# Val products of the last five batches by seven block products, sums on VectorE, last factor on GpSimd, v by casting DMAs

## Chip, cores and metric

The kernel runs on one core of one Trainium2 chip. The metric is the time of one execution on the device in microseconds (us). Engines carry the names of the profile: PE is TensorE, with PEld for its weight loads, DVE is VectorE, ACT is ScalarE, POOL is GpSimd and SP is SyncE. SBUF is the on-chip memory, PSUM the banks into which PE writes. "val" below is the product with w_val, "g" that with w_gate.

## What is computed

An attention with a sigmoid in place of the softmax, whose heads are laid side by side, and a gated feed-forward block behind it:

```python
batch, n_heads, seq, head_dim = (8, 12, 448, 64)
...
n_tokens, d_model, d_ff = (3584, 768, 1536)
...
    scores = scale * np.matmul(q, k.transpose(0, 1, 3, 2)) - np.log(S)
    attn = 1.0 / (1.0 + np.exp(-scores))
    return np.matmul(attn, v).astype(np.float32)
...
    g = x @ w_gate
    silu = g * (1.0 / (1.0 + np.exp(-g)))
    val = x @ w_val
    return (silu * val @ w_out).astype(np.float32)
```

## The kernel before

**Attention.** A block i (24 of them, 3 per batch) holds four heads. `load` (L252) brings its q, k and v in float32 into staging buffers `st`, through the DMA queue of SP. `cast_qk` (L269) makes 16-bit copies in `src`, mostly on POOL, and `cast_v` (L284) makes v in fp16 by three POOL casts; `load_v` (L293), which would load v by DMAs on POOL's queue that cast on the way, is used for i >= `VDMA`, and with `VDMA = 24` for no block. q and k are transposed into `qkT`, by PE for the first six blocks (`tr_pe`) and by a transposing DMA on SP's queue for the rest (`tr_dma`). `burst` (L387) makes one or two of a block's seven score tiles in the two PSUM buffers with the tag A, and ACT turns each into `pt` by a sigmoid. `pv` (L419) multiplies by v into two TO banks, and two copies put the result as fp16 tiles `xT` of 128 x 448 into SBUF, six per batch (768 rows of x transposed, 448 tokens).

**Feed-forward, first half.** `f1` (L461) makes, for a batch b and a block f of 128 of the 1536 hidden columns, g (six matmuls of 128 x 128 weights and 448 columns) and val (six more), each in a PSUM bank with the tag G. There are two G banks, taken in turn; for the last batch val goes to A instead. ACT takes the sigmoid of g, DVE multiplies it with g to `t1` (L482), and DVE multiplies val with t1 and a scale to `hT` (L488). Twelve f per batch, eight batches.

**Feed-forward, second half.** For each pair of batches m, `f2_set` (L608) makes the product with w_out by seven block products in place of eight (the Winograd form of Strassen's scheme): sums of hT blocks (`s`), weight sums made once by `weight_sums` (L582) in part of the staging buffers, products in TO banks (and A at the end), and adds into `osb` on DVE. `f2` (L518) makes the rest plainly. Stores go through POOL's queue while attention runs, through SP's at the end.

**Order.** The order is written out by a planner. Every step is an `Op` with an engine, an assumed duration, the steps it depends on, and the buffer tags that it takes and gives back. `list_schedule` (L64) runs through assumed time; on PE it picks the first step that is ready among the next 40, on DVE among 16, on ACT 12, on POOL 8, on SP strictly in order. Buffers of one tag are taken in the order in which the steps were listed. Each engine then executes its instructions in the order so found. In the main loop (L780 to L840) block i's attention is listed together with about one f per quarter block of the batch before and with f2 steps. `NEARLY = 5` staging buffers serve the loads after the early ones; the other six then hold the weight sums of f2.

Of the kernel before, what the change touches and what calls it, by code (L numbers as in the profile page):

```python
# [9 lines left out]
FP32 = mybir.dt.float32  # L10
FP16 = mybir.dt.float16
# [47 lines left out]
VDMA = 24  # L59
# [94 lines left out]
def kernel(  # L154
# [33 lines left out]
             "v16": 3, "qkT": 3, "pt": 10, "xT": 14, "osb": 3, "osf": 4, "S": 2}  # L188
# [6 lines left out]
    wide = one.tile([128, 512], BF16, tag="wide", name="wide")  # L195
    nc.vector.memset(wide, 0.0)
# [4 lines left out]
    NEARLY = 5  # L201
# [8 lines left out]
    stt = [stg.tile([128, 2 * NS * D], FP32, tag=f"st{n}", name=f"st{n}") for n in range(slots["st"])]  # L210

    def wsum(j, c, n=1):

        x = (j - 1) * NH + c
        o = x % 4 * HW
        return stt[NEARLY + x // 4].bitcast(FP16)[:, o:o + n * HW]
# [22 lines left out]
    def buffer(n):  # L239

        return n % len(stt) if n < uses[1] else (n - uses[1]) % NEARLY
# [5 lines left out]
    def staging(tag="st"):  # L247
        n = turns[tag]
        turns[tag] += 1
        return stt[buffer(n) if tag == "st" else n % slots[tag]]  # L250
# [168 lines left out]
    def pv(i):  # L419
# [17 lines left out]
        def fx(g):  # L437
            def fn():
                t = sb.tile([128, S], FP16, tag="xT", bufs=slots["xT"], name=f"xT_{b}_{2 * r + g}")
                cp(eng[g], t, T["pv", i, g])  # L440
                T["xT", b, 2 * r + g] = t
            return fn
# [14 lines left out]
        for g in range(2):  # L457
            R["xT", b, 2 * r + g] = op(eng[g], 0.54, fx(g), deps=[a], take=["xT"], give=[banks[g]])


    def f1(b, f):  # L461
        c, ff = divmod(f, FC)

        def mm(w, nm, j0=0, j1=KC):
            def fn():
                if j0 == 0:
                    if nm == "v" and b == B - 1:
                        T[nm, b, f] = psum.tile([128, 2, 512], FP32, tag="A", bufs=2, name="ps_vl")[:, 0, 0:S]
                    else:
                        T[nm, b, f] = psum.tile([128, S], FP32, tag="G", bufs=2, name="ps_" + nm)  # L470
                for j in range(j0, j1):
                    nc.tensor.matmul(out=T[nm, b, f], lhsT=w[c][:, j, ff * 128:(ff + 1) * 128],  # L472
                                     rhs=T["xT", b, j], start=(j == 0), stop=(j == KC - 1))
            return fn

        def fs():
            t = T["s16", b, f] = sb.tile([128, S], FP16, tag="s16", bufs=2, name="s16")
            nc.scalar.activation(out=t, in_=T["g", b, f], func=SIGM)  # L478

        def ft():  # L480
            t = T["t1", b, f] = sb.tile([128, S], FP16, tag="t1", bufs=2, name="t1")
            nc.vector.tensor_tensor(out=t, in0=T["g", b, f], in1=T["s16", b, f], op=MULT)  # L482
# [21 lines left out]
        s = op("ACT", 0.45, fs, deps=[g])  # L504
        t = op("DVE", 0.54, ft, deps=[s], give=bank)

        def val():
            vv, bank = product(wv16, "v", [g] if b or f else [])
            if f == NF - 1:
                vv.give += [x for o, _ in xs for x in o.take]  # L510
            m = b // 2
            old = R["f2", m - 2] if m >= 2 and b % 2 == 0 else []
            R["hT", b, f] = op("DVE", 0.54, fh, deps=[vv, t] + old, give=bank)
        return val

# [258 lines left out]

    f2q = []
# [4 lines left out]
    for i in range(NQ + QB + 2):  # L780
        att = i < NQ
        for sl in range(4):
# [15 lines left out]
            while len(fs) < nf and fpos < B * NF and ("xT", fpos // NF, KC - 1) in R:  # L798
                fs.append(divmod(fpos, NF))
                fpos += 1  # L800
# [41 lines left out]
    while fpos < B * NF:  # L842
        b, f = divmod(fpos, NF)
# [48 lines left out]
```

## Time and profile before

| | us |
|---|---|
| median of 3 runs | 423.64 (423.02 to 427.52) |
| the profiled execution | 423.29 |
| its span in the trace | 421.4 |
| PE busy | 412.1 (98%) |
| DVE busy | 229.5 (54%) |
| ACT busy | 218.8 (52%) |
| POOL busy | 130.0 (31%) |

The span runs from the first to the last recorded instruction; the 1.9 us between it and the execution's time lie outside. In the rows of groups, `out<-in` are the tiles' names, then come the shapes and the count, the busy time and the mean of one instruction in ns, and after the second bar the time that the engine sat idle before such an instruction and what ended it. A matmul's recorded length holds the time until its last result has left the array, so successive matmuls overlap in the records; their pace is the distance between starts.

### The profile page before, as it was taken

How to read it: one execution, taken by the hardware profiler on the slowest of the kernel's cores; microseconds unless marked ns; L12 is line 12 of the kernel's file. 1: busy time of each engine (PE TensorE's matmuls, PEld its weight loads, DVE VectorE, ACT ScalarE, POOL GpSimd, SP SyncE). 2: the span in 40 equal slices, each digit the busy share in tenths (PEclk: the TensorE clock that was granted, in tenths of full speed). 3: DMA queues.
4: the chain of work that ended last, by engine and by line, in shares of the span. 5: the costliest groups of instructions: out<-in, count | busy, mean ns of one | idle time of the engine just before them, and what ended most of it. 6: DMA issues, size and time to landing. Idle time of an engine off the chain costs nothing.

```text
span 421.4 us, 7959 instructions
## 1 busy us (share of the span) xinstructions
PE 412.1 (98%) x3215; PEld 208.0 (49%) x3217; DVE 229.5 (54%) x401; ACT 218.8 (52%) x292; POOL 130.0 (31%) x194
## 2 busy tenths in 40 slices
PE   8989899999999999999999999999999999999996
PEld 3444444444445554554554544545445545555564
DVE  3444444467676744554465564555455474673773
ACT  5997578766771155455645446544745542112000
POOL 1887845766331231414304314224100001000000
PEclk9999999999999999999999999999999999999999
DMA  8999979997871284474663745746301103021054
GB/s 273 379 376 374 375 208 340 308 321 209 221 230 54 75 207 91 146 178 106 165 165 76 185 56 195 176 87 188 59 2 37 39 2 75 2 75 35 4 148 116
DMA packets 64628, 66.97 MB, mean 159 GB/s; under 512 B 35536, under 2 KB 60752, under 8 KB 64592
## 3 DMA queue, kind: packets, MB, share of 16 engines
q1 hardware_dynamic: 62704, 59.29, 49.0%
q0 software_dynamic: 1728, 7.08, 6.5%
q8 instruction: 25, 0.41, 0.4%
q10 hardware_dynamic: 160, 0.10, 0.1%
q14 instruction: 11, 0.09, 0.1%
HBM read 47.19 MB, written 11.01 MB: 138 GB/s over the span
## 4 chain that ended last, share of the span: by engine, by line
PE 89%; DMA 9%; SPq 1%; POOL 0%; issue 0%; DVE 0%; POOLq 0%
PE ps_g L472 25%; PE ps_v L472 23%; PE ps_o L651 16%; PE ps_sc L397 8%; PE ps_pv L432 6%; DMA st<-in_moe_w_val_dram 4%; DMA st<-in_q_dram 4%; PE ps_ol L651 4%; PE ps_vl L472 3%; PE ps_o L543 2%; PE ps_ol L543 2%; SPq L261 1%; PE ps_tr L355 0%; POOL src L231 0%; DVE osb L550 0%
## 5 line engine op out<-in xcount | busy, mean ns | idle before, releaser
L414 ACT ACTIVATE pt<-ps_sc,sbiast 128x896 f16<-128x896 f32 x168 | 159.1, 1006 | 29.1 <-PE ps_sc L397 29.1
L472 PE MATMUL ps_g<-xT,wg 128*128 128x448 f16 x576 | 124.3, 353 | 0.5 <-DVE t L482 0.4
L478 ACT ACTIVATE s<-ps_g 128x448 f16<-128x448 f32 x96 | 52.2, 544 | 123.8 <-PE ps_g L472 122.8
L472 PE MATMUL ps_v<-xT,wv 128*128 128x448 f16 x504 | 109.7, 353 | 0.0
L482 DVE TENSOR_TENSOR t<-ps_g,s 128x448 f16<-128x448 f32 x96 | 59.9, 624 | 91.3 <-ACT s L478 91.0
L472 PEld LDWEIGHTS <-wg 128*128 128x128 f16 x576 | 54.7, 98 | 55.4 <-issue 8.1
L472 PEld LDWEIGHTS <-wv 128*128 128x128 f16 x576 | 52.3, 98 | 58.3 <-issue 15.9
L488 DVE SCALAR_TENSOR_TENSOR hT<-ps_v,t 128x448 f16<-128x448 f32 x84 | 52.4, 624 | 34.6 <-PE ps_v L472 33.6
L231 POOL CAST src<-st 128x896 bf16<-128x896 f32 (+1 forms) x43 | 39.8, 927 | 100.6 <-DMA st<-in_q_dram 67.2
L397 PE MATMUL ps_sc<-qkT 64*64 64x448 bf16 x672 | 51.3, 360 | 1.8 <-ACT pt L414 1.3
L231 POOL CAST v<-st 64x448 f16<-64x448 f32 (+1 forms) x72 | 41.4, 575 | 25.8 <-issue 15.7
L651 PEld LDWEIGHTS <-hT 128*128 128x128 f16 x360 | 35.2, 98 | 25.4
L667 POOL DMA_DIRECT2D out_dram<-osb x32 | 16.7, 526 | 90.4 <-DVE osb L656 90.4
L432 PE MATMUL ps_pv<-pt,v 64*64 64x448 f16 x672 | 37.1, 350 | 0.4 <-ACT pt L414 0.4
L229 DVE CAST xT<-ps_pv 128x448 f16<-128x448 f32 x40 | 23.5, 620 | 24.0 <-PE ps_pv L432 24.0
L656 DVE SCALAR_TENSOR_TENSOR osb<-ps_o,osb 128x384 f32<-128x384 f32 x56 | 30.2, 552 | 6.3 <-PE ps_o L651 6.3
L651 PE MATMUL ps_o<-wo,hT 128*128 128x384 f16 x168 | 31.9, 326 | 0.0
L397 PEld LDWEIGHTS <-qkT 64*64 64x64 bf16 x672 | 14.9, 105 | 31.1 <-issue 27.3
L432 PEld LDWEIGHTS <-v 64*64 64x64 f16 x672 | 19.6, 107 | 14.3 <-issue 3.4
L651 PE MATMUL ps_o<-st,s 128*128 128x384 f16 x120 | 22.8, 326 | 0.0
L651 PE MATMUL ps_o<-st,hT 128*128 128x384 f16 x120 | 22.8, 326 | 0.0
L651 PEld LDWEIGHTS <-s 128*128 128x128 f16 x144 | 14.1, 98 | 10.2
(45 smaller groups left out, 202.5 us busy)
## 6 DMA issues: line engine op xcount, KB each, us to landing
st<-in_q_dram SPq DMA_DIRECT2D x24, 448.0 KB, 4.3
st<-in_v_dram SPq DMA_DIRECT2D x24, 448.0 KB, 5.5
st<-in_k_dram SPq DMA_DIRECT2D x23, 448.0 KB, 4.8
out_dram<-osb POOLq DMA_DIRECT2D x36, 192.0 KB, 3.2
st<-in_moe_w_gate_dram SPq DMA_DIRECT2D x12, 384.0 KB, 9.1
st<-in_moe_w_val_dram SPq DMA_DIRECT2D x12, 384.0 KB, 8.8
st<-in_moe_w_out_dram SPq DMA_DIRECT2D x12, 384.0 KB, 6.8
out_dram<-st SPq DMA_DIRECT2D x16, 192.0 KB, 2.7
```

Of the source, the lines that this page charges most:

```text
L229: nc.vector.tensor_copy(out=o, in_=i)
L231: nc.gpsimd.tensor_copy(out=o, in_=i)
L397: nc.tensor.matmul(out=sc[64 * (g ^ a):64 * (g ^ a) + 64, a, 0:S].rearrange("k (s p) -> k s p", s=NS), lhsT=kT[r, s, 64 * g:64 * g + 64], ...
L414: nc.scalar.activation(out=pt, in_=T[("sc",) + key][:, :, 0:S], func=SIGM, bias=sb_t, scale=qkscale)
L432: nc.tensor.matmul(out=T["pv", i, a][64 * g:64 * g + 64, :], lhsT=T["v16", i][r, a, s, :], rhs=T["pt", i, s][r, a, :], start=(s == 0), sto ...
L472: nc.tensor.matmul(out=T[nm, b, f], lhsT=w[c][:, j, ff * 128:(ff + 1) * 128], rhs=T["xT", b, j], start=(j == 0), stop=(j == KC - 1))
L478: nc.scalar.activation(out=t, in_=T["g", b, f], func=SIGM)
L482: nc.vector.tensor_tensor(out=t, in0=T["g", b, f], in1=T["s16", b, f], op=MULT)
L488: nc.vector.scalar_tensor_tensor(out=T["hT", m][:, f, o * S:(o + 1) * S], in0=T["v", b, f], scalar=HSC, in1=T["t1", b, f], op0=MULT, op1=MULT)
L543: nc.tensor.matmul(out=o, lhsT=T["hT", m][:, f, t * 128:(t + 1) * 128], rhs=wo16[:, f, cs], start=(f == 0), stop=(f == NF - 1))
L651: nc.tensor.matmul(out=T["p", m, k, n], lhsT=lhs()[:, x], rhs=rhs(x), start=x == 0, stop=x == NH - 1)
L656: C[name] = op("DVE", 0.45, lambda: nc.vector.scalar_tensor_tensor(out=c(*dst), in0=T["p", m, k, n], scalar=HREC, in1=c(*other), op0=MULT, ...
```

## The change

For batches b >= `VB` = 3 the val product is made in sets. A set covers the hidden blocks f and f+6. The weights are split into two halves along the hidden blocks and two along the 768 rows; x into two halves along the 768 rows and two along the 448 tokens. In place of the eight block products (twelve matmuls of 448 columns) come seven (`ops7`; each three matmuls of 224 columns, 21 in all), by the scheme that f2 already has. `place` lists the f of these batches in the order 0, 6, 1, 7, and so on, and the set is listed behind the g of its second f.

- DVE makes four sums of x per batch (`xs`), and once, at the start of batch 3, four weight sums per set (`vs`): three go into a part of the staging memory (`vsum`), and one overwrites a block of w_val.
- The seven products share four PSUM tiles: product 1 alone, then 6 and 2, 5 and 7, 3 and 4. While attention is listed they are G banks; afterwards they are the halves of two A buffers.
- ACT copies product 1 (d0), DVE adds the others in a chain (d1, d2, d3, d4) in fp32 tiles `cv`.
- POOL multiplies the sums with t1 to hT, two products per set, in place of DVE's step at L488.
- `VDMA` goes from 24 to 11: v of blocks 11 to 23 comes by `load_v`, three casting DMAs per block on POOL's queue, in place of a load on SP's queue and three POOL casts.
- Memory is moved: all staging is one tile with 11 parts, of which 2 instead of 5 serve the later loads, the rest holding the sums; x of a batch is one tile, for two batches (before, 14 single tiles); qkT has 2 buffers instead of 3, pt 9 instead of 10, osb 2 instead of 3, the sums `S` of f2 1 instead of 2, t1 3 instead of 2.

```diff
-VDMA = 24
+VDMA = 11
+VB = 3
+HENG = "POOL"
...
     slots = {"A": 2, "TO": 2, "G": 2, "st": 11, "src": 2,
-             "v16": 3, "qkT": 3, "pt": 10, "xT": 14, "osb": 3, "osf": 4, "S": 2}
+             "v16": 3, "qkT": 2, "pt": 9, "x": 2, "osb": 2, "osf": 4, "S": 1, "cv": 2, "xs": 1, "t1": 3, "s16": 2}
...
-    wide = one.tile([128, 512], BF16, tag="wide", name="wide")
-    nc.vector.memset(wide, 0.0)
...
-    NEARLY = 5
+    NEARLY = 2
...
-    stt = [stg.tile([128, 2 * NS * D], FP32, tag=f"st{n}", name=f"st{n}") for n in range(slots["st"])]
+    NST = 2 * NS * D
+    stage = stg.tile([128, slots["st"] * NST], FP32, tag="st", name="st")
+    stt = [stage[:, n * NST:(n + 1) * NST] for n in range(slots["st"])]
+    spare = stt[:2] + [x.rearrange("p n s a d -> p (n s a d)").bitcast(FP32) for x in src16]
+    wide = wo16[:, 0, 0:512]
+    nc.vector.memset(wide, 0.0)
+    sums = stage.bitcast(FP16)[:, 2 * NEARLY * NST:]
...
-        o = x % 4 * HW
-        return stt[NEARLY + x // 4].bitcast(FP16)[:, o:o + n * HW]
+        return sums[:, x * HW:(x + n) * HW]
+
+    def vsum(j, f):
+
+        return block(4 * NH + (0, 0, 1, 0, 2)[j] * NH + f).rearrange("p (c d) -> p c d", c=KC // 2)
...
-        return stt[buffer(n) if tag == "st" else n % slots[tag]]
+        if tag == "st":
+            return stt[buffer(n)]
+        return spare[n % len(spare)]
...
-                t = sb.tile([128, S], FP16, tag="xT", bufs=slots["xT"], name=f"xT_{b}_{2 * r + g}")
-                cp(eng[g], t, T["pv", i, g])
-                T["xT", b, 2 * r + g] = t
+                if r == 0 and g == 0:
+                    T["x", b] = sb.tile([128, KC, S], FP16, tag="x", bufs=slots["x"], name=f"x_{b}")
+                cp(eng[g], T["x", b][:, 2 * r + g], T["pv", i, g])
...
-            R["xT", b, 2 * r + g] = op(eng[g], 0.54, fx(g), deps=[a], take=["xT"], give=[banks[g]])
+            R["xT", b, 2 * r + g] = op(eng[g], 0.54, fx(g), deps=[a, R.get(("xT", b, 2 * r + g - 1))],
+                                           take=["x"] if r == g == 0 else [], give=[banks[g]])
...
-                                     rhs=T["xT", b, j], start=(j == 0), stop=(j == KC - 1))
+                                     rhs=T["x", b][:, j], start=(j == 0), stop=(j == KC - 1))
...
-        s = op("ACT", 0.45, fs, deps=[g])
-        t = op("DVE", 0.54, ft, deps=[s], give=bank)
+        s = op("ACT", 0.45, fs, deps=[g], take=["s16"])
+        t = op("DVE", 0.54, ft, deps=[s], take=["t1"], give=bank + s.take)
+
+        if b >= VB:
+            R["t1", b, f] = t
+            return (lambda: val_set(b, f - NF // 2)) if f >= NF // 2 else lambda: None
...
             if f == NF - 1:
-                vv.give += [x for o, _ in xs for x in o.take]
+                vv.give += xs[0][0].take
...
-            R["hT", b, f] = op("DVE", 0.54, fh, deps=[vv, t] + old, give=bank)
+            R["hT", b, f] = op("DVE", 0.54, fh, deps=[vv, t] + old, give=bank + t.take)
...
+    def val_set(b, f):
+        KH, SH = KC // 2, S // 2
+        f2nd = f + NF // 2
+        m, o = divmod(b, 2)
+        wts = {}
+        for n, ft in enumerate((f, f2nd)):
+            c, ff = divmod(ft, FC)
+            for k in range(2):
+                wts[n, k] = wv16[c][:, k * KH:(k + 1) * KH, ff * 128:(ff + 1) * 128]
...
+        if f == 0:
+            def first():
+                T["xs", b] = sb.tile([128, 4, KH, SH], FP16, tag="xs", bufs=slots["xs"], name=f"xs_{b}")
+                tt(xsum(1), xb(0, 1), xb(0, 0), SUB)()
+            a = op("DVE", 0.51, first, deps=xs, take=["xs"])
+            R["xs", b, 1] = a
+            R["xs", b, 2] = op("DVE", 0.51, tt(xsum(2), xb(1, 1), xsum(1), SUB), deps=[a])
+            R["xs", b, 3] = op("DVE", 0.51, tt(xsum(3), xb(1, 1), xb(0, 1), SUB), deps=[a])
+            R["xs", b, 4] = op("DVE", 0.51, tt(xsum(4), xb(1, 0), xsum(2), SUB), deps=[R["xs", b, 2]])
+        if b == VB:
+            old = [x for n in range(VDMA) for x in [R["v16", n]] + R["cq", n] + R["ck", n]]
+            w = lambda n, k: lambda: wts[n, k]
+            v = lambda j: lambda: vsum(j, f)
+            R["vs", 1, f] = op("DVE", 0.36, tt(v(1), w(1, 0), w(1, 1), ADD), deps=old + [R["hT", VB - 1, NF - 1]] + ([R["vd", f - 1]] if f else []))
+            R["vs", 2, f] = op("DVE", 0.36, tt(v(2), v(1), w(0, 0), SUB), deps=[R["vs", 1, f]])
+            R["vs", 3, f] = op("DVE", 0.36, tt(w(1, 0), w(0, 0), w(1, 0), SUB), deps=[R["vs", 2, f]])
+            R["vs", 4, f] = op("DVE", 0.36, tt(v(4), w(0, 1), v(2), SUB), deps=[R["vs", 3, f]])
+        ops7 = {1: (lambda: wts[0, 0], xb(0, 0), 0, 0), 2: (lambda: wts[0, 1], xb(1, 0), 0, 0),
+                3: (lambda: vsum(4, f), xb(1, 1), 4, 0), 4: (lambda: wts[1, 1], xsum(4), 0, 4),
+                5: (lambda: vsum(1, f), xsum(1), 1, 1), 6: (lambda: vsum(2, f), xsum(2), 2, 2),
+                7: (lambda: wts[1, 0], xsum(3), 3, 3)}
...
+        tag = "A" if phase[0] else "G"
+
+        def products(ns, other=None):
+            key = ("vp", b, f, ns[0])
+
+            def fn():
+                if other and tag == "A":
+                    t = T[other, 0][:, 1, 0:S]
+                elif tag == "A":
+                    T[key, 0] = psum.tile([128, 2, 512], FP32, tag="A", bufs=2, name="ps_vl")
+                    t = T[key, 0][:, 0, 0:S]
+                else:
+                    t = psum.tile([128, S], FP32, tag="G", bufs=2, name="ps_v")
+                T[key] = t = t.rearrange("p (h s) -> p h s", h=2)
+                for h, n in enumerate(ns):
+                    for k in range(KH):
+                        nc.tensor.matmul(out=t[:, h], lhsT=ops7[n][0]()[:, k], rhs=ops7[n][1]()[:, k],
+                                         start=k == 0, stop=k == KH - 1)
...
+            a = op("PE", 0.288 * len(ns), fn, deps=xs + need, take=[] if other and tag == "A" else [tag])
+            return a, key
+
+        def cv(x, n=1):
+            return T["cv", b, f][:, x:x + n]
+
+        def add(key, dst, other, h0, n):
+            return lambda: nc.vector.scalar_tensor_tensor(
+                out=cv(dst, n), in0=T[key][:, h0:h0 + n], scalar=HSC,
+                in1=cv(other).to_broadcast([128, n, SH]) if other in (0, 4) and n > 1 else cv(other, n),
+                op0=MULT, op1=ADD)
...
+        p1, k1 = products([1])
+
+        def copy():
+            T["cv", b, f] = sb.tile([128, 5, SH], FP32, tag="cv", bufs=slots["cv"], name="cv")
+            nc.scalar.activation(out=cv(4), in_=T[k1][:, 0:1], func=COPY, scale=HSC)
+        d0 = op("ACT", 0.31, copy, deps=[p1], take=["cv"], give=p1.take if tag == "G" else [])
+        p6, k6 = products([6, 2], k1)
+        p6.deps.append((p1, LAT["PE"]))
+        d1 = op("DVE", 0.54, add(k6, 0, 4, 0, 2), deps=[p6, d0], give=p6.take or p1.take)
+        p5, k5 = products([5, 7])
+        d2 = op("DVE", 0.54, add(k5, 2, 0, 0, 2), deps=[p5, d1])
+        R["vd", f] = d2
+        d3 = op("DVE", 0.31, add(k5, 4, 3, 0, 1), deps=[d2], give=p5.take if tag == "G" else [])
+        p3, k3 = products([3, 4], k5)
+        p3.deps.append((p5, LAT["PE"]))
+        d4 = op("DVE", 0.54, add(k3, 2, 2, 0, 2), deps=[p3, d3], give=p3.take or p5.take)
+        R["p3", b, f] = p3
+        if f:
+            p3.deps.append((R["p3", b, f - 1], 0.0))
+        if f2nd == NF - 1:
+            p3.give = xs[0].take + R["xs", b, 1].take
...
+        def fh(n, ft):
+            def fn():
+                if o == 0 and ft == 0:
+                    T["hT", m] = sb.tile([128, NF, 2 * S], FP16, tag="hT", bufs=2, name=f"hT_{m}")
+                eng = nc.gpsimd if HENG == "POOL" else nc.vector
+                eng.tensor_tensor(out=T["hT", m][:, ft, o * S:(o + 1) * S],
+                                  in0=cv(1 + 2 * n, 2).rearrange("p h s -> p (h s)"), in1=T["t1", b, ft], op=MULT)
+            return fn
+        old = R["f2", m - 2] if m >= 2 and b % 2 == 0 else []
+        dur = 0.95 if HENG == "POOL" else 0.54
+        e = op(HENG, dur, fh(0, f), deps=[d4, R["t1", b, f]] + old, give=R["t1", b, f].take)
+        R["hT", b, f] = e
+        R["hT", b, f2nd] = op(HENG, dur, fh(1, f2nd), deps=[d4, e, R["t1", b, f2nd]] + old, give=d0.take + R["t1", b, f2nd].take)
...
+    def place(n):
+
+        b, p = divmod(n, NF)
+        return (b, p) if b < VB else (b, p // 2 + p % 2 * (NF // 2))
+
+    phase = [False]
...
+        phase[0] = not att
```

## The prediction

> **What bounds the kernel now.** I read the page's totals first, then the chain of waits, then the windows, then the timeline of single engines. Totals and chain:
>
> ```profile
> span 421.4 us, 7959 instructions
> PE 412.1 (98%) x3215; PEld 208.0 (49%) x3217; DVE 229.5 (54%) x401; ACT 218.8 (52%) x292; POOL 130.0 (31%) x194
> PE 89%; DMA 9%; SPq 1%; POOL 0%; issue 0%; DVE 0%; POOLq 0%
> ```
>
> TensorE is busy nearly all the time and carries 89% of the chain that ended last; the 9% of DMA lie before 45 us, where the first weights arrive. The windows say the same by stage (columns: window, its length, then busy time and instruction count of PE, weight loads, DVE, ACT, POOL, then clock, DMA share, GB/s):
>
> ```profile
> 45.00:90.00 45.00, 44.93 (x394) 20.22 (x392) 21.98 (x36) 31.67 (x41) 28.50 (x39) 1.00 1.01 298
> 165.00:208.00 43.00, 43.00 (x343) 21.78 (x341) 22.09 (x38) 23.93 (x32) 13.59 (x21) 1.00 0.63 157
> 208.00:255.00 47.00, 47.00 (x376) 23.61 (x375) 27.19 (x49) 24.71 (x33) 11.31 (x18) 1.00 0.53 123
> 255.00:303.00 48.00, 48.00 (x380) 23.98 (x379) 23.78 (x42) 27.94 (x39) 14.80 (x24) 1.00 0.57 141
> 303.00:354.00 51.00, 51.00 (x390) 25.63 (x388) 29.14 (x52) 24.73 (x34) 4.53 (x9) 1.00 0.12 30
> 354.00:396.00 42.00, 42.00 (x235) 22.89 (x234) 22.81 (x40) 8.53 (x16) 0.00 (x0) 1.00 0.12 31
> ```
>
> From 45 us on PE has no hole and full clock, while DVE is at 0.49 to 0.58 and POOL at 0.3 or less. So only PE time counts, as long as the other engines return PSUM banks in time. The last five batches start after 160 us: the product at L488 had run 36 times (three batches) by 160 us and 83 times by 354 us.
>
> **What the change takes off PE.** Before, two column blocks f and f+6 of the val product cost 2x6 matmuls of 448 columns; after, 7x3 of 224 columns, each with its own weight load. There are 5x6 = 30 such sets. The pace of a matmul is read from starts, since a row's length includes the drain (TensorE alone: start, length, instruction):
>
> ```profile
> 362.78 2.43 PE L472 MATMUL ps_g<-xT,wg 128*128 128x448 f16 x12
> 365.05 1.30 PE L472 MATMUL ps_vl<-xT,wv 128*128 128x448 f16 x6
> ```
> ```profile
> 412.78 1.14 PE L651 MATMUL ps_o<-st,hT 128*128 128x384 f16 x6
> 413.76 3.10 PE L543 MATMUL ps_ol<-wo,hT 128*128 128x384 f16 x24
> 416.70 1.15 PE L543 MATMUL ps_o<-wo,hT 128*128 128x192 f16 x12
> ```
>
> Twelve matmuls of 448 columns take 365.05-362.78 = 2.27 us, 189 ns each. Six of 384 take 413.76-412.78 = 0.98, 162.5 each. The 24 merged at 413.76 are twelve of 384 and twelve of 192 (the 192-column forms count 12 and 12): 416.70-413.76 = 2.94 less 12x0.1625 = 1.95 leaves 0.99, so 82.5 ns for 192 columns with a fresh 128x128 weight load each. By the slope between the last two (80 ns for 192 columns) 224 columns are 95.8 ns. A set falls from 2.27 to 21x0.0958 = 2.01 us; 30x0.26 = 7.8 us off PE. That is the whole gain; all else can only cost.
>
> The Trainium skill, "TensorE: Matmul & The Clock Gate", speaks against this: § LDWEIGHTS gives P/1.2 ns for P weight columns, and § Back-to-back issue gap says that the spacing is set by weight load and matmul together. If 107 ns per load were the pace, 21x107 = 2.25 us would save almost nothing, an estimate of 30x0.02 = 0.6 us. The rows above decide otherwise: the weight loads show 98 ns each, yet pairs went by at 82.5 ns, so loads overlap each other or the matmuls.
>
> **What it adds, engine by engine.** Rows of the groups by shape (mean ns after the busy time):
>
> ```profile
> L478 ACT ACTIVATE s<-ps_g 128x448 f16<-128x448 f32 x96 | 52.2, 544 | 123.8 <-PE ps_g L472 122.8
> L488 DVE SCALAR_TENSOR_TENSOR hT<-ps_v,t 128x448 f16<-128x448 f32 x84 | 52.4, 624 | 34.6 <-PE ps_v L472 33.6
> L656 DVE SCALAR_TENSOR_TENSOR osb<-ps_o,osb 128x384 f32<-128x384 f32 x56 | 30.2, 552 | 6.3 <-PE ps_o L651 6.3
> L231 POOL CAST v<-st 64x448 f16<-64x448 f32 x48 | 27.6, 575 | 2.9
> L667 POOL DMA_DIRECT2D out_dram<-osb x32 | 16.7, 526 | 90.4 <-DVE osb L656 90.4
> L637 DVE TENSOR_TENSOR hT<-hT 128x768 f16<-128x768 f16 x12 | 6.6, 551 | 0.0
> ```
>
> DVE, per set: two products at L488 leave (2x0.62); d1, d2, d4 come (448 elements from PSUM, 0.62 each) and d3 (224; with 0.16 fixed and 1.0 ns per element from the 552 and 624 rows, 0.39). Net +1.0 us. Per batch, four sums of 672 fp16 elements: between 0.48 (551 ns scaled by size) and 0.57 (not scaled); I take 0.50, so 0.35 per set. In the first of the five batches alone, 24 weight sums of 384 elements: 0.28 to 0.57, I take 0.36 (fixed part 0.16 kept), 1.4 us per set. The sets come at 2x(354-160)/47 = 8.3 us now and 8.0 after. DVE's share, 0.51 to 0.58 (4.1 to 4.7 us per set), becomes 5.5 to 6.0 of 8.0 us, hidden; in the first of the five it is 4.1+1.0+0.35+1.4 = 6.9 of 8.0, which is nearly full.
>
> ACT: one copy of 224 elements per set, about 0.36 by the 490 ns (384) and 544 ns (448) rows, on an engine at 0.5 to 0.6. Hidden.
>
> POOL: two products hT per set. No row shows a two-input operation there; it lies between the 575 ns cast of the same length and twice that, 1.15; the planner's figure in the diff is 0.95, and I take 1.0. The Trainium skill ("GPSIMD Engine Reference" § 3.1, 4497 ns for 2048 elements) would make it an estimate of 0.98. Thirteen blocks of v lose 39 casts (1.8 us a block) and gain 39 DMA issues, by the 526 ns row 1.6 us a block, up to twice that if a casting DMA of 128 rows costs more to issue. In a block of two sets (16 us) POOL goes from some 4.7 to 4.7-1.8+1.6+4.0 = 8.5 us (7 to 11 at the ends). Queued behind a waiting hT product on POOL are q and k casts, stores and v issues; a product slipping by 2 us is covered, because the third t1 buffer is wanted some 4 us later and f2 of the pair much later. v lands two blocks ahead. SP loses 13 issues.
>
> There is a price between POOL and DVE (timeline of all engines):
>
> ```profile
> 119.27 1.00 POOL L231 CAST src<-st 128x896 bf16<-128x896 f32 x1 [0.20 <-DMA st<-in_k_dram]
> 119.52 1.17 DVE L634 TENSOR_TENSOR s<-s,hT 128x768 f16<-128x768 f16 x1
> 130.80 0.55 DVE L634 TENSOR_TENSOR s<-s,hT 128x768 f16<-128x768 f16 x1
> ```
>
> The same sum takes 1.17 us when it starts inside a POOL cast and 0.55 alone. The Trainium skill ("SBUF — State Buffer" § Who interferes with whom) has this as a lock: a VectorE instruction with two SBUF inputs and a GpSimd one that reads SBUF exclude each other. By the rows, with POOL at half load each two-input sum pays 0 to 0.6, on average about 0.25; the adds from PSUM have one SBUF input and their 0.62 rows show no such spread. That puts another 1 us per set on DVE in the first of the five batches (four weight sums), so 7.9 of 8.0 there.
>
> **The banks.** While attention runs, g and val share two PSUM banks (tag G) in fixed order. From the rows: PE to consumer 0.20, handovers 0.05. Before, two f's need at least 5.2 us (g 1.14, then 0.20+0.54+0.62+handovers = 1.45 until its bank is free; twice). After: g, g to 2.28; product 1 at 2.59; products 6 and 2 at 3.73, when the second g's bank is free; 5 and 7 to 4.88; d1 ends 5.12; 3 and 4 to 5.75; d2, d3 end 6.13, and the next g may start at 6.2. So 6.2 of 8.0 us, 0.78. That compares with the stage 45 to 90 us, where the products at L488 went from 11 (by 70 us) to 23 (by 110 us), 6.7 us per two f's: 5.2 of 6.7, also 0.78, and PE was full. For the last batch val uses the A banks and the loop is gone.
>
> The smaller buffers (qkT 2, pt 9, x for two batches, osb 2, S 1, two stagings after the early loads) I cost at nothing: SP already waits for scores 132 us in total before its transposes and PE does not feel it. If that cover is gone, one attention block comes late per batch, about 1 us each. Before 45 us nothing of note changes.
>
> **Sum.** 423.3 (profiled run, 421.4 span plus 1.9 outside) - 7.8 + 1.5 for the first of the five batches (six sets at 0.25) + 1.5 for the other sets (some 0.06 each, estimate) = 418.5; the median shown is 0.35 above the profiled run, so 418.8.
>
> **Rivals.** (A) The two G banks become the bound, slower. Price: each us by which the loop passes 8.0 costs 24 us (24 sets use G). The slack is 1.8 us per set; it breaks even at 1.8+7.8/24 = 2.1 us of queueing per set, which means one whole 0.62 us operation ahead on three to four of the six DVE and ACT steps of the loop. With four of them (2.5 us) it is 0.7x24 = 17 us against 7.8: about 432. For it: DVE goes to 0.7 to 0.95. Against it: the order is planned, and 0.78 was held before. (B) DVE saturates in the first of the five batches and a tenth of a us or two is lost elsewhere: 6x0.7+24x0.1 = 6 to 7 of the 7.8 eaten, 422: within 1%. (C) The 224-column matmuls don't reach 96 ns. If they go at the 98 ns of the load rows it is still 2.06 a set and 6.3 us; only well above that is nothing gained, 424 to 426; the 82.5 ns speak against it.
>
> **Chances.** Forecast 0.46; B 0.25; C 0.03; A 0.26. This kernel's measurement tells about 1% (4.2 us) from no change. So faster by more than 1% (below 419.4) 0.46, within 0.28, slower 0.26. The forecast's own range is 415.5 (nothing eaten) to 419.4. The range of all, 415 to 431, takes in B, C and the lower half of A.
>
> **What would show it.** Right: starts of 21 val matmuls of a set sum to about 2.0 us; windows from 165 to 396 still show PE full; the last L472 work ends some 5 us earlier. Step by step: d adds at 0.62, POOL product near 1.0, DVE near 0.9 in the first of the five batches and 0.7 later. Wrong: PE idle before ps_g or the new val products, released by a DVE add (A, or B if only in that batch), or paces above 100 ns (C); or TensorE waiting for scores' or x buffers, which I cost at nothing.

## The result and the profile after

The changed kernel takes 436.69 us (median of 4 runs, 434.16 to 439.40) against 423.88 us before: ratio 1.0287 [1.0200, 1.0373], slower by some 13 us. A later set of runs on another occasion gave 435.13 us and 1.0284 [1.0270, 1.0298]. The forecast was 418.8 us with a range of 415 to 431. The profiled execution took 436.38 us with a span of 434.6 (before: 423.29 and 421.4).

The page's totals and its chain, after:

```profile
span 434.6 us, 8789 instructions
PE 411.4 (95%) x3488; PEld 233.5 (54%) x3488; DVE 287.5 (66%) x505; ACT 228.5 (53%) x322; POOL 194.3 (45%) x254
PE 20%; DVE 1%; issue 0%; DVEq 0%
```

The span is 13.2 us longer and PE is busy 0.7 us less: what is lost is not work, it is time in which TensorE stands. The chain could be followed back only through the last fifth of the span, so it doesn't say where. The windows do (same columns as before the change):

```profile
45.00:90.00 45.00, 44.50 (x381) 20.19 (x382) 20.66 (x34) 29.89 (x39) 29.12 (x40) 0.96 0.99 295
90.00:125.00 35.00, 33.43 (x289) 14.96 (x288) 22.42 (x39) 25.33 (x33) 14.60 (x20) 1.00 0.69 179
125.00:165.00 40.00, 38.61 (x256) 20.55 (x255) 24.43 (x46) 13.23 (x21) 10.12 (x17) 1.00 0.39 94
165.00:208.00 43.00, 39.87 (x353) 23.24 (x354) 32.73 (x61) 24.03 (x34) 18.36 (x24) 0.96 0.55 111
208.00:255.00 47.00, 45.10 (x412) 27.73 (x401) 37.53 (x67) 26.59 (x39) 24.22 (x29) 1.00 0.51 116
255.00:303.00 48.00, 45.85 (x418) 27.83 (x417) 33.19 (x57) 28.29 (x42) 26.67 (x35) 1.00 0.60 135
303.00:354.00 51.00, 49.39 (x452) 29.89 (x451) 39.29 (x66) 29.21 (x43) 20.32 (x24) 1.00 0.34 65
```

Where PE was full in each of these windows from 45 us on, it now lacks 1 to 3 us in nearly every one, also at 90 and 125 us, before the first of the five changed batches starts. The clock is 0.96 in two of them. DVE and POOL are far from full: DVE at 0.69 to 0.80 from 165 us on, POOL at 0.40 to 0.56.

**What the change takes off PE did come off.** The starts of val products (TensorE alone):

```profile
170.62 0.45 PE L594 MATMUL ps_v<-xs,st 128*128 128x224 f16 x3
170.91 0.45 PE L594 MATMUL ps_v<-x,wv 128*128 128x224 f16 x3
171.20 1.14 PE L782 MATMUL ps_o<-st,hT 128*128 128x384 f16 x6
```

Three matmuls of 224 columns take 0.29 us, 97 ns each. I added up, from the starts of all matmuls after 45 us, each one at the undisturbed pace of its width (189, 162.5 and 96 ns for 448, 384 and 224 columns) and called a *hole* what a start is late beyond that by over 0.15 us, slow starts at a low clock included. Val costs 104.2 us before and 96.6 after: 7.6 us less. Holes come to 0.4 us before and 18.9 after. The rest, about 1 us, is shorter delays at more changes between attention's and the products' matmuls. So −7.6 + 18.5 + 1 = 11.9; a hole at 43 us that was 1.0 us longer than before brings it to 12.9, of 13.1 measured.

**Where the holes are.** Three rows of PE's wait table:

```profile
PE ps_v L594 <- DVE t L497: 7.6, 6, 2.9
PE ps_o L782 <- ACT osb L813: 1.4, 1, 1.4
PE ps_v L487 <- DVE hT L503: 1.0, 1, 1.0
```

These are three places. The largest first, in the timeline of all engines (some rows between are left out):

```profile
192.23 2.43 PE L487 MATMUL ps_g<-x,wg 128*128 128x448 f16 x12
192.45 1.07 POOL L316 DMA_DIRECT2D v<-in_v_dram  x2
193.47 0.98 POOL L243 CAST src<-st 128x896 bf16<-128x896 f32 x1
193.50 4.02 DVE L550 TENSOR_TENSOR st<-wv,st 128x384 f16<-128x384 f16 x1
193.56 0.54 ACT L493 ACTIVATE s<-ps_g 128x448 f16<-128x448 f32 x1 [0.70 <-PE ps_g L487]
194.37 1.08 POOL L638 TENSOR_TENSOR hT<-cv,t 128x448 f16<-128x448 f32 x1
...
195.35 0.96 POOL L243 CAST src<-st 128x896 bf16<-128x896 f32 x1
196.24 1.06 POOL L638 TENSOR_TENSOR hT<-cv,t 128x448 f16<-128x448 f32 x1
197.44 1.14 DVE L497 TENSOR_TENSOR t<-ps_g,s 128x448 f16<-128x448 f32 x2
198.11 0.45 PE L594 MATMUL ps_v<-x,wv 128*128 128x224 f16 x3 [2.94 <-DVE t L497]
```

A weight sum of 384 elements, 0.35 us elsewhere, stands in the record for 4.02 us. It starts 0.03 us after a POOL cast, where POOL has just issued the DMAs of v, and ends only when POOL's run of four operations, cast, hT, cast, hT, is over. Its operands were there all along. Behind it on DVE is t, whose input s was ready at 194.1; t frees the G bank that the next val product needs; PE stands for 2.94 us. And the clock answers. In these traces it changes in steps of 3.41 us; here are the step in which most of the hole lies and the next one (same columns), and below them the same for the later run of the changed kernel, in which the hole is as long, 2.94 us:

```profile
195.74:199.15 3.41, 1.04 (x8) 0.77 (x8) 2.84 (x3) 0.90 (x3) 1.55 (x2) 1.00 0.00 0
199.15:202.56 3.41, 3.41 (x15) 1.90 (x13) 0.56 (x1) 0.76 (x1) 0.00 (x0) 0.50 0.02 5
```
```profile
196.25:199.66 3.41, 1.50 (x11) 1.05 (x11) 2.38 (x3) 0.96 (x2) 1.09 (x2) 1.00 0.00 0
199.66:203.07 3.41, 3.23 (x33) 2.11 (x31) 2.25 (x5) 1.29 (x3) 1.12 (x2) 1.00 0.15 32
```

In the first run PE stands for 2.37 us of the step, and the next step goes at a clock of 0.50, which costs up to 1.7 us more. In the second the hole is spread over two steps, 1.91 us in the one shown, and the clock stays at 1.00. Smaller holes that end with DVE's t, x or xs follow at 210, 224, 259, 276, 328, 336 and 373 us (0.65 to 1.4 us each). Summed over all sums with two fp16 inputs in SBUF, what they take beyond the shortest of their shape is 22.6 us, against 3.8 before.

Most of the sums that were late waited for one operation of POOL only. 27 are lengthened by over 0.1 us, and 24 of them got in behind the first operation, at most 0.85 us late, also where POOL's next one followed at once; the holes at 210, 224 and 276 us come behind two such sums in a row. Three waited through more: this one, one at 257.5 and one at 334.5 us, the last two through a pair of products. They make 8 of the 22.6 us. In the trace each of the three began while POOL was issuing DMAs or at the end of that.

The second place is near 95 us, in the stage of the merged weights (all engines):

```profile
94.87 2.37 POOL L352 CAST wo<-st 128x768 f16<-128x768 f32 x3
97.27 0.56 DVE L724 TENSOR_TENSOR st<-wo 128x768 f16<-128x768 f16 x1 [2.02 <-POOL wo L352]
97.75 0.62 DVE L503 SCALAR_TENSOR_TENSOR hT<-ps_v,t 128x448 f16<-128x448 f32 x1
98.42 1.30 PE L487 MATMUL ps_v<-x,wv 128*128 128x448 f16 x6 [1.02 <-DVE hT L503]
```

The first sum of output weights (L724) waits 2.02 us for the last casts of w_out, hT waits behind it on DVE, and PE behind hT. Before, the same sum ran at 91.1 us, ahead of those casts. When the changed kernel ran again, this hole was 2.95 us long, with a low clock behind it, so the profiled execution shows the place at its cheapest. The third is at 149 us, where an output buffer is wanted while its store is under way:

```profile
150.10 0.49 ACT L813 ACTIVATE osb<-ps_o 128x384 f32<-128x384 f32 x1 [7.41 <-DMA out_dram<-osb]
150.65 0.81 PE L782 MATMUL ps_o<-wo,hT 128*128 128x384 f16 x4 [1.39 <-ACT osb L813]
```

### The profile page after: what moved, and what is told of

Read it like the earlier page. It is cut to its first block, busy times and chain, and to the rows that moved or that the text cites. A ratio compares the mean times of both kernels' runs of the same rounds, so it can differ in the third digit from the quotient of the medians.

```text
span 434.6 us, 8789 instructions
## 1 busy us (share of the span) xinstructions
PE 411.4 (95%) x3488; PEld 233.5 (54%) x3488; DVE 287.5 (66%) x505; ACT 228.5 (53%) x322; POOL 194.3 (45%) x254
## 5 line engine op out<-in xcount | busy, mean ns | idle before, releaser
L487 PE MATMUL ps_g<-x,wg 128*128 128x448 f16 x576 | 122.3, 353 | 1.6 <-DVE t L497 1.2
L493 ACT ACTIVATE s<-ps_g 128x448 f16<-128x448 f32 x96 | 52.3, 545 | 93.1 <-PE ps_g L487 91.1
L638 POOL TENSOR_TENSOR hT<-cv,t 128x448 f16<-128x448 f32 x60 | 65.0, 1101 | 68.0 <-DVE cv L605 67.9
L243 POOL CAST src<-st 128x896 bf16<-128x896 f32 (+1 forms) x43 | 41.2, 961 | 44.4 <-DMA st<-in_q_dram 26.4
L605 DVE SCALAR_TENSOR_TENSOR cv<-ps_v,cv 128x448 f32<-128x448 f32 (+1 forms) x92 | 51.8, 564 | 13.0 <-PE ps_v L594 8.8
L487 PE MATMUL ps_v<-x,wv 128*128 128x448 f16 x216 | 48.3, 360 | 1.0 <-DVE hT L503 1.0
L594 PEld LDWEIGHTS <-wv 128*128 128x128 f16 x360 | 34.3, 98 | 14.5 <-issue 11.3
L241 DVE CAST x<-ps_pv 128x448 f16<-128x448 f32 x40 | 23.7, 617 | 14.7 <-PE ps_pv L446 14.7
L487 PEld LDWEIGHTS <-wv 128*128 128x128 f16 x216 | 19.6, 99 | 24.2 <-issue 9.7
L594 PEld LDWEIGHTS <-st 128*128 128x128 f16 x270 | 24.8, 98 | 13.0 <-issue 7.7
L503 DVE SCALAR_TENSOR_TENSOR hT<-ps_v,t 128x448 f16<-128x448 f32 x36 | 22.5, 624 | 13.0 <-PE ps_v L487 11.8
L594 PE MATMUL ps_v<-x,wv 128*128 128x224 f16 x138 | 21.0, 262 | 7.4 <-DVE t L497 7.4
```

The lines of the kernel that those rows point to most:

```text
L243: nc.gpsimd.tensor_copy(out=o, in_=i)
L594: nc.tensor.matmul(out=t[:, h], lhsT=ops7[n][0]()[:, k], rhs=ops7[n][1]()[:, k], start=k == 0, stop=k == KH - 1)
L605: return lambda: nc.vector.scalar_tensor_tensor(out=cv(dst, n), in0=T[key][:, h0:h0 + n], scalar=HSC, in1=cv(other).to_broadcast([128, n, ...
L638: eng.tensor_tensor(out=T["hT", m][:, ft, o * S:(o + 1) * S], in0=cv(1 + 2 * n, 2).rearrange("p h s -> p (h s)"), in1=T["t1", b, ft], op=MULT)
```

## The experiments

Two theories at first: **Lock** (the holes come from DVE's two-input sums, held by POOL, with t behind them) and **Banks** (rival A: DVE and the G banks are simply overloaded by the sets). A third came in with the first run: **Memory** (the smaller and moved buffers). Ratios are against the kernel before, run on the same chip.

**Parts of the change alone.** No sets, the rest of the change in place:

```diff
-VB = 3
+VB = 8
```


> The changed kernel without any set: all eight batches make val by twelve matmuls and hT on DVE as before; kept are the smaller buffers, the one staging tile and v of blocks 11 to 23 by casting DMAs. Theory (POOL's products and casts shut DVE's two-input sums out, and PE waits for the next g's bank): no hT on POOL and no xs or weight sums, so the holes of PE behind 160 us go; 424 to 428 us, with the holes before 160 us (about 5 us, from the small buffers and the start) still there. Rival 1 (the smaller buffers and the v DMAs cost most): 432 to 437 us. In both the 7.8 us of PE are given up.

Measured: 430.65 us, 1.0149 [1.0107, 1.0192]. A miss for what I held: without one block product of the sets, 7 us are lost. In its trace the two-input sums are nearly undisturbed (2.4 us in all); the holes are the one near 95 us (3.4 us, and 2.9 more at a low clock), the one near 150 us (1.56) and one of 1.0 us at 231 us. So the memory side is a cause by itself.

The last factor back on VectorE, sets kept:

```diff
-HENG = "POOL"
+HENG = "DVE"
```


> The changed kernel with hT of the sets made by DVE in place of POOL (60 products of some 0.6 us move). Theory of the lock: POOL has 65 us less that can shut DVE out, the sums on DVE lose most of their 22.6 us of lengthening and the PE holes that follow them go; 425 to 430 us. Rival 2 (DVE simply has too much work, 0.66 of the span busy): DVE gains 36 us and loses at most 22, so PE waits more; 440 to 450 us.

Measured: 432.02 us, 1.0176 [1.0132, 1.0219], some 3 to 4.7 us better than the changed kernel although DVE has 60 more products. The sums' lengthening falls from 22.6 to 4.7 us and the holes between 165 and 303 us from 9.6 to 5.7. That speaks for Lock and against Banks, though Lock had forecast 425 to 430: outside that stretch holes of 8.0 us are left (9.3 in the changed kernel), 3.6 of them near 99 us.

A tiny POOL memset ahead of and behind each product hT, to let a waiting sum in:

```diff
+    gapt = one.tile([128, 8], FP32, tag="gapt", name="gapt")
...
+                nc.gpsimd.memset(gapt, 0.0)
...
+                nc.gpsimd.memset(gapt, 0.0)
```


> The changed kernel with a tiny memset on POOL before and after each hT product, nothing else. If a waiting DVE sum is passed over only because POOL's next operation follows at once, the memset (which reads nothing) lets it in: the sums of 2.5 to 4.0 us shrink to 1.1 to 1.3 at most and one or two of the PE holes (3.1, 1.4, 1.3 us) shrink with them; 431 to 435 us. If each single POOL operation is the price, or DVE's load, nothing changes: 435 to 438 us.

Measured: 433.68 us, 1.0228 [1.0190, 1.0265], 1.5 to 3 us better than the changed kernel and in the 431 to 435 forecast for a sum that is let in. The same place in its trace, POOL's rows and then DVE's:

```profile
193.47 0.98 POOL L244 CAST src<-st 128x896 bf16<-128x896 f32 x1
194.34 0.15 POOL L639 MEMSET gapt<- 128x8 f32 x1
194.41 1.08 POOL L640 TENSOR_TENSOR hT<-cv,t 128x448 f16<-128x448 f32 x1
195.38 0.14 POOL L642 MEMSET gapt<- 128x8 f32 x1
```
```profile
193.50 4.15 DVE L551 TENSOR_TENSOR st<-wv,st 128x384 f16<-128x384 f16 x1
```

Here the sum is passed over all the same: one memset stands between a cast and a product, and the next operation always begins before the last has ended. At the other two long holds, two memsets stand between two products, and the second product begins 0.15 us after the first has ended. There the sum gets in behind the first. The one at 257.5 us, in the changed kernel and then here:

```profile
257.54 2.52 DVE L768 TENSOR_TENSOR hT<-hT 128x768 f16<-128x768 f16 x1
```
```profile
255.89 1.57 DVE L771 TENSOR_TENSOR hT<-hT 128x768 f16<-128x768 f16 x1
```

The third goes from 2.91 to 1.97 us. So one memset between is no opening, and two in a row were one at both places; the largest hold stays, and with it most of the time.

v by casting DMAs in the kernel before, and nothing else:

```diff
-VDMA = 24
+VDMA = 11
```


> The kernel before with v of blocks 11 to 23 by casting DMAs on POOL's queue, all else as before. Theory of the lock: the DMAs cost nothing and POOL has less to do; 421 to 425 us. Rival 1 with the v DMAs as the culprit: 428 us or more.

Measured: 424.02 us, 1.0004 [0.9979, 1.0029]. This part is free.

**Where the sums' area lies.** The merged output weights reuse staging buffers once the early loads are done. Before, they start at buffer 5 of 11, after at buffer 2. There are 69 uses before the buffers turn over, so the last load of w_out (number 68) lands in 68 mod 11 = buffer 2. The kernel before with that alone moved (and the output buffers of its end put elsewhere, to be free):

```diff
-    NEARLY = 5
+    NEARLY = 2
...
-        return stt[buffer(n) if tag == "st" else n % slots[tag]]
+        return stt[buffer(n) if tag == "st" else (0, 1, 8, 9)[n % 4]]
```


> The kernel before with v by casting DMAs (which alone cost nothing) and NEARLY = 2: the weight sums of f2 lie in staging buffers 2 to 7 instead of 5 to 10, two buffers serve the later loads, and the four output buffers of the end are 0, 1, 8 and 9. The last load of w_out goes to buffer 2. Theory of the place: the first weight sum, which stands on DVE ahead of an hT product, has to wait for the cast of that last load; a PE hole of some 3 us near 95 us, a lower clock for some us behind it, 428 to 431 us. Rival (one of the other small buffers makes that hole): no hole near 95 us, 423 to 425 us.

Measured: 430.58 us, 1.0167 [1.0145, 1.0189]: 6.6 us above the kernel that it is made from. All engines near 95 us in its trace:

```profile
94.83 2.37 POOL L338 CAST wo<-st 128x768 f16<-128x768 f32 x3
...
97.24 0.56 DVE L593 TENSOR_TENSOR st<-wo 128x768 f16<-128x768 f16 x1 [5.88 <-POOL wo L338]
97.71 0.62 DVE L482 TENSOR_TENSOR t<-ps_g,s 128x448 f16<-128x448 f32 x1
...
98.38 0.91 PE L472 MATMUL ps_g<-xT,wg 128*128 128x448 f16 x2 [4.81 <-DVE t L482]
```

The place alone makes the hole: 4.8 us of PE, and 1.9 more at clocks of 0.56 and 0.76. Now the other way round: in the kernel without sets and in the changed kernel, the two sum areas exchange places, so that the early output sums lie behind buffer 2 and the val sums, wanted later, on it:

```diff
+        x += 3 * NH
...
-        return block(4 * NH + (0, 0, 1, 0, 2)[j] * NH + f).rearrange("p (c d) -> p c d", c=KC // 2)
+        return block((0, 0, 1, 0, 2)[j] * NH + f).rearrange("p (c d) -> p c d", c=KC // 2)
```


> The kernel of e1_no_sets with the two areas of sums exchanged, so that f2's weight sums lie in the upper staging buffers (about 6 to 10), as before the change. Theory of the place: the hole near 95 us and the low clock behind it go; what stays is the hole of 1.6 us near 150 us (two osb buffers) and one of 1 us; 424.5 to 426.5 us. Rival: 429 to 432 us as in e1_no_sets.

> The changed kernel with the two areas of sums exchanged, nothing else. Theory of the place: the hole near 97 us goes, and 2 to 5 us with it; the holes behind 190 us, which theory gives to POOL's lock, stay: 431 to 434 us. If the place explained all: 424 to 428 us.

Measured without sets 426.08 us, 1.0063 [1.0045, 1.0081]: 4.6 us back, and of the holes above 1 us only the one of 1.5 us at the output buffer is left. With sets 432.19, 1.0206 [1.0184, 1.0229]: 3 to 4.5 us back. So the place is worth 3 to 7 us, differing with the size of the hole and the clock behind it, and the other moves of memory 2.5 (f2 against before), of which 1.5 are the hole at the output buffer. What is left between f2 and f3, 6.1 us, is the sets' own balance: 7.6 us less of products, and 13.7 lost (the holes differ by 13.5).

**The lock itself.** The plan is told of it: two-input sums on DVE and operations on POOL that read SBUF exclude each other when the order is made; its figures for hT (1.05), for three sums (0.47) and for the landing of a store (2.9) are taken from the trace:

```diff
+    held = {"POOL": 0.0, "DVE": 0.0}
...
+                if o.lock:
+                    r = max(r, held["DVE" if e == "POOL" else "POOL"])
...
+                if o.lock:
+                    held[e] = now + dur
```


> f3_sums_high with a planner that knows of the lock: a DVE sum with two SBUF inputs and a POOL operation that reads SBUF are never planned at the same time, hT on POOL is planned with 1.05 us, and a store of f2 frees its buffer 2.9 us later. The instructions are the same, their order differs. Theory of the lock: the lengthening of the sums falls from some 20 us to under 8, the holes of PE behind 190 us and the one near 150 us shrink by more than half; 421 to 427 us. Rival (DVE has too much work, whatever the order): 430 to 434 us.

Measured: 423.54 us, 0.9995 [0.9975, 1.0015]: 8.65 us below f3. The holes fall from 16.0 to 7.4 us; the hole at the output buffer is gone too. Sums are still lengthened by 16.9 us in all, since the plan is not binding in time, but none beyond 2.91.

The same with the order made binding: where the plan puts a POOL operation that reads SBUF behind a DVE sum (by less than 4 us), it waits for that sum's semaphore:

```diff
+        if o.lock and o.eng == "DVE":
+            held = traced[len(traced) - 1], o.t0
+        elif o.lock and o.eng == "POOL" and held and o.t0 < held[1] + 4.0:
+            tc.add_manual_dep(traced[n0], held[0].name, mybir.DependencyInfo(
+                mybir.DependencyClass.Sync, mybir.DependencyReason.DATA), reason="lock")
```

and beside it the changed kernel once more, the f4 plan with the last factor on VectorE, and g1 with three durations nearer to the trace:

> The changed kernel itself, beside the others on the same chip. All theories: 433 to 438 us, with the hole near 97 us, the one near 150 us and the holes behind 190 us; it tells how much of the profiled 2.6 us hole and low clock near 45 us is of that execution alone.

> f4_lock_plan, and each POOL cast or product also waits for the DVE sum that was planned before it (within 4 us). The same instructions in the same order; 24 or so more waits on POOL. If a sum is passed over because POOL's next operation takes the lock first, no sum is lengthened by more than one POOL operation (1.3 us at most, total under 9 us), and the holes of 1.3 us near 193, 217 and 325 us shrink: 419 to 422.5 us, faster than the kernel before. If DVE's amount of work makes them, 423 to 425 us.

> f4_lock_plan with hT of the sets on DVE. POOL then shuts DVE out seldom, but DVE has some 33 us more to do. Theory of the lock with a good order: nothing more to gain from moving hT, and DVE's load costs: 424 to 428 us. If POOL's products were the only trouble, whatever DVE does: 419 to 423 us.

> g1_order with the planner's durations of the sets' ACT and DVE steps nearer to the measured pitch (0.95, 0.52, 0.58, 0.34 us). If what is left is drift between plan and execution, 417 to 420 us; if not, as g1_order within 1 us.

Measured: the changed kernel 435.13 us; g1 **420.78 us, 0.9946 [0.9934, 0.9959]**, below the kernel before; g2 423.77, 1.0009 [1.0000, 1.0018]; g3 421.43, 0.9951 [0.9936, 0.9966], the same as g1 within the intervals. g2 is no better than f4 (423.54), so once the plan knows the lock, nothing is gained by taking hT off POOL. g3 misses the 417 to 420 forecast for it: durations nearer the trace gain nothing. The page of g1 and its windows from the first changed batch on:

```profile
span 419.0 us, 8796 instructions
PE 407.6 (97%) x3488; PEld 232.7 (56%) x3488; DVE 272.9 (65%) x505; ACT 227.7 (54%) x322; POOL 191.4 (46%) x254
```
```profile
165.00:208.00 43.00, 42.22 (x392) 25.73 (x391) 32.86 (x68) 26.93 (x39) 23.23 (x31) 1.00 0.66 141
208.00:255.00 47.00, 46.83 (x430) 28.89 (x428) 35.46 (x66) 26.46 (x39) 25.04 (x32) 1.00 0.54 129
255.00:303.00 48.00, 46.63 (x438) 28.55 (x437) 29.79 (x57) 28.61 (x43) 24.88 (x34) 1.00 0.64 134
303.00:354.00 51.00, 51.00 (x456) 32.52 (x454) 38.49 (x72) 25.66 (x40) 18.70 (x23) 1.00 0.21 42
```

The same POOL operations are done, with POOL at 0.52 to 0.54 in the first three of these windows, and PE is nearly full. Sums are lengthened by 6.4 us, none held beyond 1.18. The holes are 4.7 us, 1.5 of them at 257 us where ACT's copy of a val product stands behind one of an output waiting for its store.

**Which of the two did it.** f4 without the rule, only its durations; f3 with the waits alone, in its own order and with its own durations; and g1 with a guard of 0.1 us behind each sum and a longer landing of stores:

> f4_lock_plan without the planner's rule on the lock: what stays are the later freeing of a store's buffer, 1.05 us for hT on POOL and 0.47 us for three sums of f2. Theory of the lock: only the hole near 150 us goes for sure; 428 to 432 us, sums lengthened by 15 us or more. Rival (any better durations and a fresh order mend it, the lock matters little): 422 to 426 us.

> f3_sums_high in its own order and with its own durations, but each POOL cast or product waits for the DVE sum that was planned before it (within 4 us). Theory of the lock with passing over: the sums of 2.5 to 4.0 us fall to 1.3 at most, the total lengthening from 23.6 to under 14, the holes behind 190 us shrink by a third to a half: 426 to 430 us. Rival (the order alone is to blame): 431 to 434 us.

> g1_order with 0.1 us of room between a sum and a POOL operation in the plan, and a store's buffer freed 4.0 us later instead of 2.9. If what is left in g1_order (holes of 0.6 near 192 and 1.5 us near 257) is drift of the plan and a store that lands late: 418.5 to 420.5 us; else 420 to 422 us.

Measured: h1 431.59 us, 1.0175 [1.0130, 1.0220], with 23.1 us of lengthening and sums held up to 4.03 us again: the rule is worth 8 us. What the durations alone are worth, 431.59 against f3's 432.19, lies within the spread of h1's runs (429.1 to 433.3). h2 422.95 us, 0.9980 [0.9963, 0.9996], 9.2 us below f3, more than the 426 to 430 that I thought possible without a new order. The wait table of PE for the same pair of tiles, f3 and then h2:

```profile
PE ps_v L595 <- DVE t L498: 7.4, 6, 2.9
```
```profile
PE ps_v L599 <- DVE t L502: 0.9, 2, 0.5
```

Nothing was taken off any engine there, some POOL operations only start later; holes in all fall from 16.0 to 7.1 us and no sum is held beyond 1.4. h3 missed: 423.31 us, 0.9990 [0.9974, 1.0007], 2.5 above g1, with holes of 2.1 us from 157 to 161 us at output copies and 1.1 us at 217. Why its order falls out worse is open.

## Why the prediction was wrong

**What the change takes off PE: right.** 7.8 us were forecast, 7.6 measured; 224 columns go at 97 ns with a weight load each, so rival C is out. Worked out from the Trainium skill's figure for a load ("TensorE: Matmul & The Clock Gate" § LDWEIGHTS), 107 ns is an estimate for each of these, and it is no pace here; the measurement decides.

**The single operations: right.** hT on POOL, taken as 1.0, is 1101 ns; d adds 621 and 390 ns (0.62 and 0.39); the ACT copy 357 ns (0.36); a val weight sum 347 ns and a sum of x 491 ns where nothing holds them (0.36 and 0.50). The 0.39 for the sum of 224 elements was partly luck: the two rows named for it give 0.12 fixed and 1.13 ns per element, so 0.37. "v by casting DMAs" cost nothing (e4). Two rows of after (groups by shape) show the first two:

```profile
L638 POOL TENSOR_TENSOR hT<-cv,t 128x448 f16<-128x448 f32 x60 | 65.0, 1101 | 68.0 <-DVE cv L605 67.9
L605 DVE SCALAR_TENSOR_TENSOR cv<-ps_v,cv 128x448 f32<-128x448 f32 x69 | 42.9, 621 | 12.3 <-PE ps_v L594 8.8 <-ACT pt L428 0.4
```

**"Each two-input sum pays 0 to 0.6, on average about 0.25": the step that failed most.** The average was right: 22.6 us over 104 such sums are 0.22 us each, though three of them make a third of it. The bound was not, and the average is not what the path feels. I read the lock as a queue of one: a sum waits for the POOL operation that is running, then goes. The trace bears that out for 24 of the 27 lengthened sums, with up to 0.85 us in place of 0.6; the other three were held through two to four operations, up to 3.7 us beyond their own time. I then charged the price to DVE's load, 7.9 of 8.0 us in the first of the five batches, and asked whether that is full; DVE was at 0.76 there. What counts is one long hold, or two short ones in a row: whatever is behind the sum on DVE comes late as a whole, here t, which frees a G bank, or a sum of x that PE itself wants. My sum had 3.0 us for all queueing of the sets; f2 to f3 show 13.7, of which h2 gives back 9.2 by its waits alone. What the other 4.5 us are is not shown.

**"The smaller buffers I cost at nothing": failed too.** I named the scores' and x buffers as what could be late, and these were not. I left out the placing, NEARLY from 5 to 2, though it is in the diff: f1 shows 6.6 us for it alone, e1 to f2 4.6. And the two output buffers cost 1.5 us at 149 us. Together e1 shows 7.1 us that the sum had at 0. The question to ask of a reused buffer was which load has it last.

**The banks, rivals.** Rival A (the two G banks, about 432 us) came nearest in time and sign, and the sign that I had named for it is in the trace: PE idle before the new val products, released by DVE, though by t and not by an add. "PE full from 165 to 396" is wrong: 221.3 of 231 us. But A's mechanism, one 0.62 us operation ahead on three or four of six steps, is not what happened: g1 has the same banks, sets and operations and reaches 420.78. Its break-even, 2.1 us of queueing per set, was exceeded in single sets by a single hold. The bank order holds when nothing is held, as forecast: PE is at 51.00 of 51.00 in g1's last window above.

That the bare sum of 418.5 is the time of a kernel without holds and with the buffers well placed is argued and not shown: no run reached it. g1, with 4.7 us of holes left, comes within 2.0 us of the forecast. The clock was not in my sum at all.

**What is shown and what is not.** By experiment: the placing (f1, f2), the sums held by POOL (e2, h1, h2, f4), the price of v (e4). Only read from the trace: that the hole at 149 us is the output buffer's; it goes when the plan knows how long a store takes (f4, and h1 without the rule) and stays where only the waits are added (h2), but in h1 too that was one of three durations. A hole at 43 us (2.6 us and a low clock after it, against 1.6 before) was 0.85 us when the same kernel ran again, so it is chance. Not settled: what lets POOL pass a waiting sum. In the kept traces 14 of the 15 sums that were passed over began during or right behind a DMA issue of POOL, but many that began so went at their own time, and no run changed those issues alone.

## What to carry to other kernels

When work moves to GpSimd beside VectorE sums with two inputs in SBUF, don't charge an average share of the overlap: look for runs of back-to-back GpSimd operations, take one operation as the usual hold and the whole run as its bound, and see who is behind the sum. If the sum must go first, make GpSimd wait for it; that was worth 9 us here at no cost in work. And when a buffer area moves, look up which transfer uses each part of it last, before calling it free.

## What the runs showed of the hardware

- **A waiting sum can be passed over.** The Trainium skill, "SBUF — State Buffer" § Who interferes with whom, calls the shared ports "an exclusive lock", in which a VectorE instruction with two SBUF inputs contends with a GpSimd instruction that reads SBUF. The exclusion agrees with these traces. Who is next it leaves open: a sum that starts 0.03 us into a cast waited through three further GpSimd operations that started after it (0.35 us became 4.02), with one memset between them as well (4.15). Most lengthened sums, 24 of 27, got in after one operation. An explicit wait of GpSimd ended the long holds (at most 1.4 us in h2, 1.18 in g1).
- **The clock falls after a step with a pause in it.** The clock of these traces goes by steps of 3.41 us. Behind steps in which PE stood for 2.0 to 3.2 us (nine cases in after, e1, e2, e3, f1, f3, g0 and h1) the next one went at 0.50, which costs up to 1.7 us; behind steps with 1.9 us or less it stayed at 1.00. So a pause of 2.94 us cost a slow step in one run and none in another of the same kernel.
- **Weight loads are hidden down to 192 columns.** Matmuls with a fresh load of 128x128 each go at 189, 162.5, 96 to 97 and 82.5 ns for 448, 384, 224 and 192 columns. That is one line, 0.417 ns a column and 2.5 ns more, though the record of a load is 98 ns.
